# Batch 2's last three units: k, q and u transposed by transfers as well, with a new order of all work

## The chip, the cores and the metric

The kernel runs on one core of a Trainium2 chip. The metric is the device time of one execution in microseconds (us), here the median of three runs: 161.28 us before, from 160.6 to 162.63. The profile is of one further execution.

## The reference

Two layers follow each other. The first is a gated linear attention over 4 batches, 8 heads, 768 tokens and 48 channels; its state is a 48 x 48 matrix for each head. The second takes its output as x of 768 tokens by 384 channels and mixes tokens by a rank of 32, then channels by a hidden layer of 1536:

```python
for t in range(S):
    state = alpha[:, :, t, :, None] * state + np.einsum('bhd,bhe->bhde', k[:, :, t], v[:, :, t])
    y[:, :, t] = np.einsum('bhd,bhde->bhe', q[:, :, t], state)
...
h = xt @ U @ V
u = x + h.transpose(0, 2, 1)
ch = np.maximum(u @ w_ch1, 0.0) @ w_ch2
return (u + ch).astype(np.float32)
```

Inputs and output are float32; the kernel multiplies in bf16.

## The kernel before

**Tiling.** The 768 tokens of a batch are cut into six chunks of 128; a unit is one chunk with all heads, or, in batch 0 and in the first four units of batch 1, a pair of chunks with half of the heads. Batches are counted from 0, so the third batch is batch 2. All units of batches 2 and 3 are of the plain kind (`stage_gla`).

**A plain unit.** Four loads of 192 KB bring alpha, k, q and v (L339). ACT takes the logarithm of alpha (L534), PE sums it along the tokens by a triangular matrix (L541, with totals at L543), and ACT makes the running product and its inverse (L551, L552). DVE or POOL multiply k and q by them (L562) into one `rkq` buffer of bf16. The products are then transposed, since the scores need channels on the partitions. Normally PE does it (L576, four transposes for k and four for q, into PSUM) and DVE or ACT copy the result into a `kqt` buffer (the copies are recorded in the helper, L273 and L275). For units in `QUEUE_T`, all six of batch 3, one transposing transfer on SP's queue goes from `rkq` to `kqt` instead (L588). Then come scores (L604), the causal mask on DVE (L614), the state's new term (L627), its addition on DVE (L654) and scaling (L638), and y from old state and masked scores (L666, L671), for which v has been cast to bf16 (`rv`, L277 or L273). y is copied into `xb`.

**After the six units of a batch** (`stage_mix`): the low-rank mix (L686, L716) and u = x + h on DVE (L717). The hidden layer needs u with channels on the partitions. For batches 1 and 2 PE transposes it for two chunks at a time (L736, six transposes) and DVE or ACT copy it out. For batches in `QUEUE_U`, only batch 3, a transposing transfer does it for two chunks (L722); u then lies chunk by chunk, and `u_half` gives the first layer three pieces of 128 columns where it has one of 384 otherwise. The hidden layer is `mlp1` (L767, relu at L777 and L779) and `mlp2` (L793, addition of u at L799), after which the output is stored (L802, L804).

**Order.** No planner runs on the chip or at build time: `TABLE` lists all groups of instructions in one order, three characters each, two for the number of the group and one for its engine (P, A, D, G for POOL, S for SP). Each engine and SP's queue execute their own entries in this order, waiting where data or a buffer is missing. `SLOTS` gives the buffers, in the order of first use. An entry `++x` issues so many matmuls on a filler, to warm PE; the table before has none. All loads, stores and transposing transfers are issued by SP.

**Buffers.** There are 40 `io` buffers for loads and results, 4 `rkq`, 4 `kqt`, 5 `rv`, and 8 banks of PSUM.

Of the kernel before, what the change touches and what calls it, by code (L numbers as in the profile page):

```python
# [13 lines left out]

CODE = "ABCDEFGHIJKLMNOPQRSTUVWXYZabcdefghijklmnopqrstuvwxyz0123456789+-"
TABLE = """
A8SCcACePCfABISBASCzAC1PA9SBQSETAEVPCiDCkPA+SCgACjDClPCnDDjADlPC2ABDSCmDC3AEXAC0GA-SCdGC4ADmACoPCqDDoACrPChACsDBBSC5GDCP
DDDDnAABSCpDEWAC7PC9ACvPCtPCuDDEPBCSC6GC8PC+DBESDKAAFGAGPAHAAJPAKAEYADFDC-PDBDDADDMPDOADNACwPCyADPABJSDpGDrPBMSBKSDtDDGP
DqGDZPBSSEaGDsPDuDBFSEcPEeDDHPDIDDvPDwDDxDBHSDLADQGDSPDyPDUDD8ACxAD+PBLSDkADzPD0DDJADaPDbDBRSEZGEbPEdDBYSG2ABGSDRGEAAD-A
BUSGfAG4PG6ABTSEUAEBAG5AD1PD2DDcPDdDDTPDVDBNSECGD3PEfPEhDGhPGiAEgDGkABOSEDGBPSD9GD4PBVSGlGBWSGjAGmGBgSBcSBXSGgGAASADGBZS  # L20
G8GAQSARGAMSANGAOSAPGAeSAfGEiPD5PD7AG7AD6AEjPEkDDWPDXDDYDDfPAgSELPEmPDePEEPEGDAhGEFPElPEHAEMPENDAiSAjGEnPEpDEoAHmABbSG3G
AUSAVGBaSG9GBiSASSATGAWSBkSBdSDgPDhDDiAHNAEIPEJDBoSGnPGpAEOPEPPEKDBfSHoPHqAHtGHrABeSHpAAYSBhSAaSAcSAmSAoSAqSBqSBjSBpSAkS
BmSBlSBnSAuSAwSAsSAySA2SA4SBrSGoPGqDHPPEQPERAESAGuPGvDGwDGrPGtDGsDEqPACSBySA6SA0SEwPErPEzPE8PE5PEtPEsAE9PE+AE6PE7AE2PFHP
EuPEvAE3PE4DE0PE1AExPEyDG+PFJPFDPE-PFjPHAAGxGFFPFKDHRAFNPHQAHSAFkDFGDFlPFBPFCDFIDFnPFoAFfPFgAF5PF6DFdPFOAFmAFEDFADFeDFhP
GyPFiAF3PBwSB0SG-PHBAF1PBsSBuSHFPF4DHGDAXAGzPG1DG0AF2AH-AHCPHEDHDDHHDIVAFLPFMDFTPFUDFRPFSDIBPFtPFuAICAHTGHVPHXAFVPFrPFsA
HJPFWAIFAAdAHOGHvPHxDHcPHdDHKPHLDIXPIYAIZAIDAHMAHeDHfDHUGHWPFpPFqAHYDFPPFQAAZGIEAHsGHuPHwDAbGFZPAnGFxPFyAFaDHyPHZPHbDHaD
H0DHzDFbPFcAIHDAlAFXPFYABvSHiPFvPFzPHhPHIGApGIbGFwAF0AArGALGIdPHjPHlDHkAHnGH1PH2DH3DH4DIaGIfAIcPIeAH6PGTPIJPILDIGGIIPIAA
H7PIKDGNPH8PH+AH9AIMPIODINDIgPIiDIhDGZPAxAF7PIPPAvGAzGAtAGaPH5GIRDGBPHgGITPIQDISDGCPIWAIjPGOPGUPIUAIkAAEGIlPA1GImDF8PA7A
A5AA3AGDPGEDItPIzPI1PI0DB4SBtSF9PIvPIuDF+DKLAI2DIwDGVPInPIpPK0AK2PGPPKfAKNPKRAKQAIxPGWDK3AI3PI4AGbPIoDIqDKhPKkAKiAIrPIyD
JXPJjPGcDIsAKjAKnDKlAGQDJTPJUAJkAI7PJNPJJPJDPJEDKOAKSDK5AK4AI8AKPAKMGKTGJHPI5PJdPI6AK6AJKDJIDJLPJODJYDB2SBxSBzSJMALJAJVP  # L30
JWAJRPJSAK8GKpPKrAJfPLLPLPAK+PLAAKbPJeDB1SKUPKWAK7DJgDB8SLeALNALOALMAJBPKmGKoPKgGKvPKcDKwDKVPKXDI-PJPPJnPJoDJlPJAAJmAK9P
I9PI+AJFPJGAJQALgPLhALjALkAKqDJCDK-DKYPKZDLBPKsPKtDLDDCASB+SLzACBSB9SJZPJaALiAKBPB5SCQSLQDKuDLCDKaDB7SCESGHPJvPL1PJbPLmG
LoPLqDJhPKxDJwPNlANnPB3SK1GLEPLFDJxPGIPLHPJyDJiDGJPGKDOaAL3AJcAL2AL4DNpAB6SLRGLTPLVDNrANoANqALSPLUAB-SLfGCCSCGSNtDKyPKzA
LKALlGLnPJ7PL5GLIDLpDL7PL9AL6PL8ALGGLZPLaDCTSObGKCPLrPLtDLWPLXDL+PCHSNmAKDPKEDLsDLYDKdPKeDJ8PCISN2AN4PN5AN6AN8AN7AOcPOdA
J9PJ+DCFSNsGAIGNyPLbGLxPLuPNzDJpPLvDLwGL-DJ1PCMSCDSL0GCJSGRSLyAOIAOKPKGPOMACLSN3AOgAOOALcPMADMBPLdDMCDJqPNuSCSSN9DNvPNxD
NwDMDPONAJrPKHPMEAMNPOfAOeAMFPMGDMLPMMDCYSOiGCUSO+AJ2PMHPCWSCPSCKSCRSOhGCNSCVSCOSCbSO-GMIDN0PKIPN1AOsAMODMRPMJPMKAMPPMQD
JsDJ3PKJDMTPMUDODPOEDJtSMfPMhPMiDMjPMgAMkAOLAOJAMbPMnPMlPMSDMVPOPDJ4DMWDOuPOwAO0DOyAMcDPAPOxAMXPMYAMxPPBAMoAMyAMdPMeAMvP
OQDNBPCZSNCAM3POVPMwDOFDOWDMZPOvAOzGCXSN+GMpPMqDMaDOnPM9PM+DOXDM1PPCAMmANDPM7PM8AOjSOkPOoDM5PM6AM-PNAANFPNHPCaSM2AOmDOlD
OqPOrDMtPNEDNIPORSOSPMuAN-SOAPOCDOBDM4AMzPM0AOTDNRPMrPMsAOGPOHANSPOUDO1SO2PO3DO4DPEGPDGNGAPFSPGPNMPOpGOtGO5PO6DO7GNJPO8P
O9ANTPOYPOZAPHDJzSGSSPIDPJPPKANbPGLSPLPPMANcPPNPPZPPaDPODNWPPPPPQDPSPPRSPTDNNPPUPPVDPWSNgPNOPNhPPXPNXPGMSPYDPbSNiPNjDNYP  # L40
NZDF-SNdPNeDPsPPiPPoPPyPPzANfSNKDNLSKFSPjDGFSGGSJ5SPePPfAPcPPgPPhAP0PP1APpDNUDJuSNVSNaSP2PP3DQEPPqPPtAQAPQBDQFAP4PPmPPnA
P+PP-APdAJ6SPuPKKSNPDKASNQSPwPQCPPxDQIPPrAGdSPkPPlDP5DGASQRPQWPP8PQMPP6PQDAPvAQXPQSPP7DQbPQNPQTPQUDQVSGeSJ0SQGPQKPQYPQZD
QOPQPDQqPQlPQLAQJAP9DQrPGXSJ-SQmPNkSQaSQQSGYSQHAQsPQtDQuSQnPQoDQcPQpSQgPQdPQeDQfSQhPQiPQjDQkS
"""
SLOTS = """
AAAABCBBDECCADFAEAAFBGBCAHBACGHABBECAIBDABAAFBHJBKBDGDFEBBBBAACLCDMNCGCODEPFDHDBCQCAEFACHRDACDDSGTAUACVBBCWEABEXBFCGAAAB
YZBDaCbBcdeAfAghijHCBEGBAkCDBHBFEBlCmDnACDEBFAGHCGFCCEHDADDICJKLNOQPMRSTUVWXYZacbdBAGFAAHBADefgCEGFBAADHGFBDEACABGAAAFEA
CEHACGhiEFjkBDCABBHEBBCGBACFBBEDHDGBEBBAFAEDACADABHAEFBDGEHCAACFlCBHAAECFGBBBCBDHAACBFEBGBACCFDGBBCAAAGBmCAGBnABDAACBDCG
CBCCHBADACBHEBBFFBCAFHBDACADECHGBGHBCFADDEGBABBICAJABBHFEDCAEABCDEGACACFDAHEGABCKNCLOBAFQMCPRGBECBACHBBDTCABASUACCDAVCBD
BEWBXaADCABHGDEDCAYCDACGBBECZEdAfCGABAFCbgDABABGBCAHcjDiBBDChBBDAEAlDCACEAAAECCeCACFkBnGIHJKAEAACFCEQRAFAEGADBDAEFGBMDAA  # L50
CCBHAGBANEHABGCTBADDHACFCBGADAFDVBGBBAHDGBACCEBCAGABCCBHCCEFBDGAAFBGBHAAFGAAHGAWOXHAGFBLBDAFYGEBAFHGEPACHGDBAGFCaEFZfDBg
cFj
"""


# [91 lines left out]
def kernel(  # L147
# [13 lines left out]
    B, H, S, D = q.shape  # L161
# [16 lines left out]
        return [const.tile(shape, dtype, name=f"{name}{i}") for i in range(n)]  # L178

    PAIRS = {0: 3, 1: 2, 2: 0, 3: 0}  # L180
    QUEUE_T = tuple((3, c) for c in range(6))
    LAST, CUT = 3, 240
    QUEUE_U = (3,)
    P = Plan()
    nc.scalar.preload_act_table_set("natural_log_exp_and_others")

# [160 lines left out]
    def xk(b, xb, c):  # L347
        return [(xb, c, 0), (xb, c, 1)] if paired(b, c) else [(xb, c)]
# [182 lines left out]
    def stage_gla(b, c, sprev, xb):  # L531
# [37 lines left out]
        kT, qT = Part(kqT, 0), Part(kqT, 1)  # L569
        if (b, c) not in QUEUE_T:  # L570
            tk, tq = Buf(bank), Buf(bank)
# [12 lines left out]

        if (b, c) in QUEUE_T:
            P.add(
# [93 lines left out]
    def stage_mix(b, xb, ub, uT):  # L680
# [33 lines left out]
        for c in range(NC):  # L714
            hb = Buf(bank)
            P.add({"PE": mm(DM)}, lambda e, c=c, hb=hb: nc.tensor.matmul(hb()[:, 0:DM], lhsT=(ve_sb if paired(b, c) else vm_sb)[:, c * C : (c + 1) * C], rhs=utx(), start=True, stop=True), r=[utx, ("ve" if paired(b, c) else "vm", c // NT)], w=[hb])  # L716
            P.add({"DVE": 465}, lambda e, c=c, hb=hb: nc.vector.tensor_tensor(ub()[:, c, :], xb()[:, c, :], hb()[:, 0:DM], op=ALU.add), r=[hb] + xk(b, xb, c), w=[(ub, c)])  # L717
            if b in QUEUE_U:
                if c % 2 == 1:
# [28 lines left out]
    def u_half(uT, ct, tt, by_chunk):  # L748
        if not by_chunk:
            return uT()[:, ct, tt * TW : (tt + 1) * TW]  # L750
        flat = uT().rearrange("p j t -> p (j t)")
        return flat.rearrange("p (c j t) -> p c j t", c=NC, j=NCT)[:, tt * NT : (tt + 1) * NT, ct, :]

    def mlp1(b, uT, h1, tt):
        for jt in range(NJ):
            hb = Buf(bank)

            if b == 0:
                need = [(uT, tt, j) for j in range(NCT)]
            elif b in QUEUE_U:  # L760
                need = [(uT, "c", c) for c in ((0, 1), (1, 2))[tt]]
# [3 lines left out]
            def f(e, jt=jt, hb=hb):  # L765
                for ct in range(NCT):
                    nc.tensor.matmul(  # L767
                        hb()[:, 0:TW], lhsT=w1_sb[:, ct, jt * 128 : (jt + 1) * 128],
                        rhs=u_half(uT, ct, tt, b in QUEUE_U), start=(ct == 0), stop=(ct == NCT - 1),
                    )  # L770
# [87 lines left out]
```

## Time and profile before

| | |
|---|---|
| median of three runs | 161.28 us (160.6, 161.28, 162.63) |
| profiled execution | 162.81 us, its span 161.0 us |
| TensorE clock granted | full in the span |
| busy: PE, DVE, ACT, POOL | 150.4, 110.1, 90.4, 59.4 us |
| DMA: packets, MB | 96964, 31.05 |
| HBM read and written | 23.89 and 4.72 MB, 178 GB/s |

The span runs from the first to the last instruction recorded; the execution's time has what lies around it as well. A row of the list of groups has line, engine, operation, tiles, shapes and count, then busy time and the mean of one, then the engine's idle time ahead of such instructions with what ended it. A matmul's busy time (some 320 ns for 384 columns) contains its passage through the array; matmuls follow each other faster, so their own share is read from the chain, where consecutive groups are laid end to end. "SPq" is SP's queue: the time in which it is issuing a transfer. "Landing" is from a transfer's issue to its completion.

### The profile page before, as it was taken

The page shows a single profiled execution, that of the slowest core. Times are in us where ns is not written, and L with a number is a line of the kernel's source. Part 1 is how long each engine was busy: PE and PEld are TensorE (multiplying, and loading weights), DVE is VectorE, ACT ScalarE, POOL GpSimd, SP SyncE. Part 2 cuts the span into 40 slices and gives each one's busy share as a digit, 9 for nine tenths or more (in the row PEclk, how much of TensorE's full clock was granted, in tenths as well). Part 3 has the DMA queues.
Part 4 walks back from the last instruction along what each step waited for, and adds up shares of the span by engine and source line. Part 5 has one row for each costly group of instructions (what it writes and reads, how often), then busy time and mean ns, then how long its engine had stood idle before and what let it go on. Part 6 is the DMA issues. An engine that isn't in the chain of part 4 may idle for free.

```text
span 161.0 us, 4539 instructions
## 1 busy us (share of the span) xinstructions
PE 150.4 (93%) x1740; PEld 100.6 (62%) x1740; DVE 110.1 (68%) x242; ACT 90.4 (56%) x233; POOL 59.4 (37%) x95
## 2 busy tenths in 40 slices
PE   0599999999999999999999899999999999999991
PEld 0386877666657655667667575766566566556561
DVE  6157898789768819576888996898868358341431
ACT  4476978766687264989875475468434301560300
POOL 8087686766785321053088431213902000000000
PEclk9999999999999999999999999999999999999999
DMA  5999999898999999899979999878661047751274
GB/s 138 268 299 279 261 278 239 254 310 217 289 249 270 220 222 217 166 210 223 216 154 201 176 183 216 172 155 154 122 125 30 0 93 200 238 162 44 83 235 147
DMA packets 96964, 31.05 MB, mean 193 GB/s; under 512 B 90640, under 2 KB 96912, under 8 KB 96944
## 3 DMA queue, kind: packets, MB, share of 16 engines
q1 hardware_dynamic: 96944, 30.78, 81.6%
q8 instruction: 13, 0.21, 0.6%
q14 instruction: 7, 0.06, 0.1%
HBM read 23.89 MB, written 4.72 MB: 178 GB/s over the span
## 4 chain that ended last, share of the span: by engine, by line
PE 61%; DMA 13%; SPq 11%; DVE 6%; ACT 4%; issue 2%; POOL 0%; DVEq 0%; ACTq 0%; POOLq 0%
PE ps L793 25%; PE ps L767 21%; SPq L332 11%; DMA io<-in_k_dram 4%; DMA io<-in_v_dram 3%; DMA io<-in_alpha_dram 3%; DMA io<-in_moe_w_ch_dram 3%; PE ps L604 2%; PE ps L716 2%; PE ps L671 2%; PE ps L541 1%; PE ps L736 1%; ACT h1t L777 1%; DVE pm L446 1%; PE ps L686 1%
## 5 line engine op out<-in xcount | busy, mean ns | idle before, releaser
L793 PE MATMUL ps<-w_sb,h1t 128*128 128x384 bf16 (+2 forms) x300 | 54.0, 319 | 0.0
L767 PE MATMUL ps<-uT,w_sb 128*128 128x384 bf16 x288 | 52.2, 326 | 0.1
L777 ACT ACTIVATE h1t<-ps 128x384 bf16<-128x384 f32 x62 | 28.5, 497 | 29.0 <-PE ps L767 28.9
L767 PEld LDWEIGHTS <-w_sb 128*128 128x128 bf16 x288 | 26.7, 98 | 16.5 <-ACT w_sb L273 0.4
L793 PEld LDWEIGHTS <-h1t 128*128 128x128 bf16 x300 | 27.0, 97 | 15.9 <-issue 1.0
L779 DVE TENSOR_SCALAR h1t<-ps 128x384 bf16<-128x384 f32 x34 | 17.9, 553 | 9.9 <-PE ps L767 9.9
L799 DVE TENSOR_TENSOR io<-ub,ps 128x384 f32<-128x384 bf16 (+2 forms) x25 | 13.2, 535 | 9.5 <-PE ps L793 9.0
L614 DVE TENSOR_TENSOR pm<-ps,maskc 128x512 bf16<-128x512 f32 x28 | 17.7, 684 | 2.3 <-PE ps L604 2.3
L717 DVE TENSOR_TENSOR ub<-xb,ps 128x384 bf16<-128x384 bf16 x24 | 12.2, 549 | 5.4 <-PE ps L716 5.4
L446 DVE TENSOR_TENSOR pm<-ps,maskp 128x512 bf16<-128x512 f32 x20 | 12.9, 686 | 2.7 <-PE ps L435 1.4
L562 POOL TENSOR_TENSOR rkq<-io,aa 128x384 bf16<-128x384 f32 x9 | 8.3, 926 | 17.3 <-ACT aa L552 7.3
L277 POOL CAST rv<-io 128x384 bf16<-128x384 f32 x15 | 8.4, 558 | 14.0 <-DMA io<-in_v_dram 14.0
L273 ACT CAST xb<-ps 128x192 bf16<-128x192 f32 (+1 forms) x23 | 8.5, 390 | 5.2 <-PE ps L671 4.3
L275 DVE COPY kqt<-ps 128x512 bf16<-128x512 bf16 x22 | 9.1, 419 | 3.0 <-PE ps L411 2.9
L562 POOL TENSOR_TENSOR rkq<-io,ai 128x384 bf16<-128x384 f32 x8 | 7.6, 951 | 7.6 <-DMA io<-in_q_dram 5.3
L277 POOL CAST w_sb<-io 128x384 bf16<-128x384 f32 x16 | 8.0, 505 | 5.8 <-DMA io<-in_moe_w_ch_dram 5.8
L273 ACT COPY kqt<-ps 128x512 bf16<-128x512 bf16 x14 | 8.0, 598 | 3.3 <-PE ps L576 1.7
L393 POOL TENSOR_TENSOR rkq<-io,ai 128x384 bf16<-128x384 f32 x9 | 8.2, 911 | 4.4 <-DMA io<-in_k_dram 2.3
L371 PE MATMUL ps<-lt,upto 128*128 128x384 bf16 x10 | 4.1, 410 | 5.9 <-ACT lt L362 5.8
L534 ACT ACTIVATE lt<-io 128x384 bf16<-128x384 f32 x14 | 7.2, 535 | 3.0 <-DMA io<-in_alpha_dram 3.0
L411 PE MATMUL ps<-ident,rkq 128*128 128x128 bf16 x80 | 8.8, 251 | 0.0
L638 POOL TENSOR_TENSOR st<-sm,tot 128x384 bf16<-128x384 f32 x5 | 4.1, 828 | 12.5 <-DVE sm L654 12.5
(113 smaller groups left out, 232.0 us busy)
## 6 DMA issues: line engine op xcount, KB each, us to landing
io<-in_alpha_dram SPq DMA_DIRECT2D x24, 192.0 KB, 3.7
io<-in_k_dram SPq DMA_DIRECT2D x24, 192.0 KB, 3.7
io<-in_q_dram SPq DMA_DIRECT2D x24, 192.0 KB, 4.0
io<-in_v_dram SPq DMA_DIRECT2D x24, 192.0 KB, 3.9
io<-in_moe_w_ch_dram SPq DMA_DIRECT2D x24, 192.0 KB, 3.9
out_dram<-io SPq DMA_DIRECT2D x13, 192.0 KB, 1.9
out_dram<-io SPq DMA_DIRECT2D x20, 96.0 KB, 2.2
out_dram<-io SPq DMA_DIRECT2D x1, 120.0 KB, 1.7
```

The lines of the kernel that those rows point to most:

```text
L273: nc.scalar.copy(dst, src)
L277: nc.gpsimd.tensor_copy(dst, src)
L332: lambda e: nc.sync.dma_start(t().rearrange("p (h j) d -> p h (j d)", j=2), src[b, hs, sl, :].rearrange("h (p j) d -> p h (j d)", j=2)),
L446: nc.vector.tensor_tensor(dst, s2, maskp.to_broadcast([C, 2, 2, C]), op=ALU.mult)
L562: eng.tensor_tensor(dst()[:, :, 0:D], a(), x(), op=ALU.mult)
L614: nc.vector.tensor_tensor(pm()[:, :, par, :], s2, maskc.to_broadcast([C, HP, C]), op=ALU.mult)
L717: P.add({"DVE": 465}, lambda e, c=c, hb=hb: nc.vector.tensor_tensor(ub()[:, c, :], xb()[:, c, :], hb()[:, 0:DM], op=ALU.add), r=[hb] + xk( ...
L767: nc.tensor.matmul(hb()[:, 0:TW], lhsT=w1_sb[:, ct, jt * 128 : (jt + 1) * 128], rhs=u_half(uT, ct, tt, b in QUEUE_U), start=(ct == 0), sto ...
L777: nc.scalar.activation(dst, hb()[:, 0:TW], AF.Relu)
L779: nc.vector.tensor_scalar_max(dst, hb()[:, 0:TW], 0.0)
L793: nc.tensor.matmul(hb()[:, 0 : hi - lo], lhsT=h1()[:, jt, c * C : (c + 1) * C], rhs=w2_sb[:, jt, lo:hi], start=(jt == 0), stop=(jt == NJ - 1),
L799: P.add({"DVE": 468}, lambda e, hb=hb, lo=lo, hi=hi: nc.vector.tensor_tensor(flat(ou)[:, lo:hi], ub()[:, c, lo:hi], hb()[:, 0 : hi - lo], ...
```

## The change

The units 3, 4 and 5 of batch 2 join `QUEUE_T`, and batch 2 joins `QUEUE_U`. For these PE's transposes and the copies out of PSUM are gone, and six more transposing transfers are issued by SP: three from `rkq` to `kqt`, three from `ub` to `uT`. The first hidden layer of batch 2 reads u by chunks. The order of all groups and the buffers are new throughout, and four warming matmuls stand in it, all among its first 40 entries.

```diff
 TABLE = """
-A8SCcACePCfABISBASCzAC1PA9SBQSETAEVPCiDCkPA+SCgACjDClPCnDDjADlPC2ABDSCmDC3AEXAC0GA-SCdGC4ADmACoPCqDDoACrPChACsDBBSC5GDCP
...
+BQSA8SCcAETACePBISDjADlP++BA9SCfACiDCkPDoA++CA+SBDSChACgACjDClPCnDBASDmACzAC1PCmDCoPC4ABJSBKSA-SCdGCrPC3ABCSC6DC0GEVP++B
...
-    QUEUE_T = tuple((3, c) for c in range(6))
+    QUEUE_T = tuple((b, c) for b in (2, 3) for c in range(6) if b == 3 or c > 2)
     LAST, CUT = 3, 240
-    QUEUE_U = (3,)
+    QUEUE_U = (2, 3)
```

Read out of the tables, SP's queue has these entries, one after the other, around the new transfers (b is the batch, T and U are the transposing transfers for k with q and for u, the figure is the unit, for U the second of its two chunks):

```
before, entries 103 to 112:  v b3.0 | alpha b3.1 | k b3.0 | alpha b3.2 | v b2.5 | k b3.1 | store | v b3.1 | T b3.0 | q b3.3
after, entries 100 to 112:   k b2.5 | q b3.0 | v b3.0 | k b3.0 | alpha b3.3 | T b2.4 | T b2.5 | T b2.3 |
                             k b3.2 | alpha b3.4 | v b2.5 | T b3.0 | k b3.1
after, entries 117 to 124:   q b3.4 | U b2.1 | U b2.3 | v b3.2 | q b3.3 | U b2.5 | q b3.2 | k b3.4
before, entries 126 to 131:  T b3.3 | q b3.5 | T b3.2 | T b3.1 | T b3.4 | T b3.5
after, entries 126 to 136:   q b3.5 | k b3.5 | T b3.2 | T b3.3 | v b3.3 | T b3.4 | T b3.1 | v b3.4 | T b3.5 |
                             store | v b3.5
```

PE's entries ahead of y of unit 5 of batch 2 (the group of L666 and L671) are in number:

| PE's groups ahead of it | before | after |
|---|---|---|
| transposes of k and q in plain units | 16 | 10 |
| `mlp1` groups of three matmuls | 48 | 48 |
| `mlp2` groups of four matmuls | 30 | 27 |
| state's new term in plain units (L627) | 7 | 6 |
| all other groups | the same | the same |
| warming matmuls | 0 | 4 |

## The prediction

> **What bounds the kernel now.** I read the page first: busy shares, the slices, the chain that ended last.
>
> ```profile
> span 161.0 us, 4539 instructions
> ...
> PE 150.4 (93%) x1740; PEld 100.6 (62%) x1740; DVE 110.1 (68%) x242; ACT 90.4 (56%) x233; POOL 59.4 (37%) x95
> ...
> PE   0599999999999999999999899999999999999991
> ...
> DMA  5999999898999999899979999878661047751274
> ...
> PE 61%; DMA 13%; SPq 11%; DVE 6%; ACT 4%; issue 2%; POOL 0%; DVEq 0%; ACTq 0%; POOLq 0%
> ```
>
> PE is full from the third slice to the last but one, so a removed matmul should be worth its own time. But the DMA row is as full as PE's until slice 28, about 112 us. Two resources are at their limit together for two thirds of the span. The windows, by stage, say the same:
>
> ```profile
> 0.00:6.00 6.00, 1.14 (x9) 0.87 (x10) 2.74 (x24) 2.71 (x4) 3.27 (x15) 1.00 0.67 169
> 6.00:60.00 54.00, 52.27 (x814) 36.97 (x813) 39.81 (x89) 38.64 (x105) 33.91 (x52) 1.00 1.01 263
> 60.00:112.00 52.00, 51.28 (x547) 34.53 (x545) 42.65 (x84) 36.02 (x95) 16.94 (x22) 1.00 0.99 189
> 112.00:134.00 22.00, 21.91 (x221) 13.38 (x219) 14.43 (x26) 6.32 (x15) 5.26 (x7) 1.00 0.38 77
> 134.00:158.00 24.00, 23.78 (x159) 14.84 (x156) 10.24 (x21) 6.70 (x15) 0.00 (x0) 1.00 0.56 169
> ```
>
> The columns are stretch, length, busy time of PE, PEld, DVE, ACT and POOL, then granted clock, DMA share and GB/s. From 6 to 112 us the DMA share is 1.0; only then does it fall to 0.38. The clock is full throughout. PE goes in the order of the list, so a load that lands after PE has reached its reader stops PE even where other work would be ready.
>
> **What is removed.** PE loses six groups of four k/q transposes and three groups of six u transposes.
>
> ```profile
> 64.10 0.69 PE ps L736 x12
> ...
> 65.68 0.36 PE ps L736 x6
> ...
> 72.38 0.22 PE ps L576 x4
> ...
> 91.86 0.65 PE ps L793 x4
> ...
> 93.69 0.17 PE ps L627 x4
> ...
> 97.15 0.20 PE ps L671 x8
> ```
>
> In the chain a k/q group takes 0.22 us and a u group 0.36 (12 matmuls take 0.69, so 0.345 to 0.36). The sum is 6 x 0.22 + 3 x 0.345 = 1.32 + 1.03 = 2.35 us of PE time. PE is at its limit there, so that is the most that the removal itself can give.
>
> Nine evacuations go as well:
>
> ```profile
> L275 DVE COPY kqt<-ps 128x512 bf16<-128x512 bf16 x22 | 9.1, 419 | 3.0 <-PE ps L411 2.9
> L273 ACT COPY kqt<-ps 128x512 bf16<-128x512 bf16 x14 | 8.0, 598 | 3.3 <-PE ps L576 1.7
> L275 DVE COPY uT<-ps 128x768 bf16<-128x768 bf16 x3 | 1.7, 556 | 0.7 <-PE ps L736 0.7
> L273 ACT COPY uT<-ps 128x768 bf16<-128x768 bf16 x3 | 2.4, 799 | 0.2 <-PE ps L736 0.2
> ```
>
> At 0.42 or 0.60 us six times, and 0.56 or 0.80 three times, that is 4.2 to 6.0 us of DVE and ACT. Neither bounds this stretch (42.65 and 36.02 of 52 us), so I cost it at nothing. What it could give is the wait that PE has on DVE around 90 us, in this row:
>
> ```profile
> 88.00:92.00 4.00, 3.55 (x57) 2.48 (x55) 3.97 (x8) 2.42 (x6) 2.43 (x3) 1.00 1.34 201
> ```
>
> There DVE is full and PE lacks 0.45 us; that is the bound, from nothing to -0.45.
>
> The first layer now reads batch 2's u by chunks. Batch 3 does so in the kernel before:
>
> ```profile
> 104.14 2.92 PE ps L767 x18
> ...
> 134.35 9.75 PE ps L767 x60
> ```
>
> Batch 2's matmuls (the upper row) and batch 3's (the lower) both take 0.162 us each: nothing. The four 512-column warming matmuls stand among the first entries of the list, where PE works 1.14 of 6 us: nothing; if that cover failed they would cost about 0.22 us each, an estimate from 0.162 us for 384 columns, together 0.9.
>
> **What is added.** Six transfers on SP's queue, three for k and q and three for u. Before has nine of that kind:
>
> ```profile
> L588 SPq DMA_TRANSPOSE kqt<-rkq x6: 1232/1256/2921, 89.4 to 117.2; - x6
> ...
> DMA to landing us min/median/max: 3.1/3.2/4.8
> ```
>
> ```profile
> L722 SPq DMA_TRANSPOSE uT<-ub x3: 1232/1252/1264, 129.4 to 132.7; - x3
> ...
> DMA to landing us min/median/max: 2.8/2.8/2.8
> ```
>
> On a quiet queue each holds SP for 1.25 us and lands after 2.8 to 3.2. Most of the nine run after 109 us, when the queue is quiet. The one that ran amid the loads is the interesting one:
>
> ```profile
> 83.96 0.73 SPq L339 DMA_DIRECT2D io<-in_k_dram  x1
> 84.79 1.13 SPq L339 DMA_DIRECT2D io<-in_alpha_dram  x1
> 86.01 0.87 SPq L339 DMA_DIRECT2D io<-in_v_dram  x1
> ...
> 88.58 0.54 SPq L339 DMA_DIRECT2D io<-in_v_dram  x1
> 89.36 2.92 SPq L588 DMA_TRANSPOSE kqt<-rkq  x1
> ...
> 106.32 1.97 SPq L588 DMA_TRANSPOSE kqt<-rkq  x1
> ```
>
> It held SP for 2.92 us, where loads beside it hold it for 0.54 to 1.13, and it is the one with the landing of 4.8. The transfers' own rate fell with it:
>
> ```profile
> 84.00:88.00 4.00, 4.00 (x60) 3.04 (x58) 2.89 (x7) 2.05 (x7) 3.24 (x6) 1.00 1.04 207
> 89.40:94.20 4.80, 4.35 (x76) 3.13 (x75) 4.77 (x10) 2.47 (x8) 1.03 (x2) 1.00 1.05 147
> 94.20:98.20 4.00, 4.00 (x58) 2.66 (x55) 3.49 (x8) 2.35 (x8) 1.27 (x2) 1.00 1.15 223
> ```
>
> 147 GB/s against 207 and 223 around it: over 4.8 us some 0.33 MB were not moved, about 1.5 us of the stream, beside the 0.26 MB that the transposition itself is. So among loads one costs from 1.25 to 2.92 us of SP's queue. The second that had loads close by, at 106.32, took 1.97. I take 2.0 and keep both ends.
>
> By the Trainium skill, "Advanced Engine Details and Errata", section "X-Bar Transpose (TRN2)", transposing transfers are as fast as ordinary ones, some 90% of a plain copy. By that rule the three would cost what their bytes cost, near 1.25 us; the trace agrees on the quiet queue and not at 89.36 us (2.92).
>
> **Where it lies on the path.** In the new list the three k/q transfers are the 105th to 107th entry of SP's queue: behind them wait the loads of k and alpha of two units of batch 3, and then v of batch 2's last unit. In both lists 106 loads are ahead of that v; in the new one also the three transfers. Before, it was issued at 86.01 and used by the L671 group of the chain at 97.15, 11 us later. That distance is what shrinks, from both sides.
>
> PE gets there sooner: counting the groups ahead of this one in both lists, the new has the six k/q groups less (1.32), three mlp2 groups less, which now come behind it (3 x 0.65), and one group of L627 less (0.17): 3.4 us. Unhindered PE is there at 97.15 - 3.4 = 93.7.
>
> The v gets there later:
>
> ```profile
> io<-in_v_dram SPq DMA_DIRECT2D x24, 192.0 KB, 3.9
> ...
> L277 POOL CAST rv<-io 128x384 bf16<-128x384 f32 x15 | 8.4, 558 | 14.0 <-DMA io<-in_v_dram 14.0
> ```
>
> Issue at 86.0 + 3 x 2.0 = 92.0, landing after 3.9, cast 0.5: usable at 96.4, so PE stands **2.7 us**. At 1.25 us apiece it is usable at 94.2 (0.5 us late); at 2.92 at 99.2 (5.5 us late). The readers of the transposed k and q of units 3 and 5 stand 3.4 and 3.1 us of PE work ahead of the same point and fall in the same wait, since their transfers take the places from 83.96 on (the 105th entry before), 2 us apart, and land 3.2 to 4.8 later.
>
> The transfers' own waits: unit 5's needs the kqt buffer that unit 1 frees 9.2 us of PE work before the point, unit 3's that of unit 0, 8.4 before, so at about 84.9 and 85.5; their turns on SP come at 83.96 + 1.25 = 85.2 or later. Unit 5's k is the 100th load, four ahead; its scaled copy is there some 0.6 us before its turn. I cost both at nothing; if the scaling is late, every load behind waits on SP, since SP goes in order.
>
> The u transfers: the first two must land before the first layer of batch 2. In the new list 4.7 us of PE work lie between the last sum they need and that layer; 0.16 + 0.55 for sum and addition plus a landing of 2.8 to 4.8 gives 3.5 to 5.5. Cost 0, at most 0.8. They hold SP while they wait for the additions, and the loads of batch 3 (v of unit 2, q of unit 3) wait behind them; batch 3 has room for that as long as v of its last unit arrives. That v is now issued behind the last k/q transfer: 1.25 + 0.5 + 3.9 + 0.5 = 6.15 us after it, against 6.0 us of PE work between the buffer that starts the transfer and its reader. Cost 0, at most 1.0 with a slower landing.
>
> **The sum.** On the profiled execution (162.81 us, of which the span is 161.0): -2.35 + 2.7 = +0.35, so 163.2 and a span of 161.4. The median of the runs, 161.28, is 1.5 lower than that execution; I put the difference on the median: **161.6 us**. The three runs lie between 160.6 and 162.63, so 2% (3.2 us) is about what a measurement of this kernel can tell from no change.
>
> **The rivals.**
> *The transfers cost no more than on a quiet queue.* Then 1.25 apiece, a stall of 0.5: 161.28 - 2.35 + 0.5 = 159.4. For it speak seven of the nine transfers, which took near 1.25; against it that the one at this very place in the stream was the slow one.
>
> *The queue in front of the loads decides (slower).* All three take 2.92 and land in 4.8: a stall of 5.5, and with the u transfers' 0.8 and the last v's 1.0 a total of 7.3 - 2.35 = +5, or 166.3. The place is SP's queue ahead of batch 2's last v; it loses time from 1.9 us a transfer on (stall 2.35) and more than 2% from a total stall of 5.6, that is at 2.9 us a transfer, or 2.4 with the two late terms. For it: the row at 89.36, and a DMA share of 1.0 up to 112 us, which leaves no gap to catch up in. Against it: the loads' own issue times are partly back-pressure, which three transfers in a row may share.
>
> *The new order is better at the start as well.* PE lacks 4.9 us in the first 6 and 1.7 in the next 54. If the new order of loads wins 1.4 of these 6.6 and rival one holds: 158.0. Nothing in the profile says which way a new order goes; it can as well lose as much.
>
> **How the numbers follow.** Forecast (160.2 to 163.3): 0.45. Quiet-queue price (158.4 to 160.2): 0.24. Queue decides (163.3 to 167): 0.24, two thirds of it above 164.5. Better start (below 158.4): 0.07. Faster by over 2% is below 158.05: most of the last, and a little of the second, 0.08. Slower by over 2% is above 164.5: 0.17, and 0.03 for a wait that I did not find: 0.20. The rest, 0.72, is within 2%. The range from 158.6 to 165.2 leaves out about 0.08 below and 0.12 above.
>
> **What would show it.** PE's matmuls fall by 42 less the four warming ones, to 1702, and the L576 and L736 rows shrink to 40 and 18. The three k/q transfers of batch 2 show 1.3 to 2.9 us on SP, and the load rate dips beside them. PE has an idle gap of 2 to 3 us between 86 and 97, released by DVE masks behind a transfer or by the cast of v; later PE is full to the end. I am wrong on the price if the three take 1.25; wrong on the mechanism if PE has no gap there and the time is lost or won before 60 us or after 112, in batch 3.

## The result, and the profile after

The changed kernel takes 163.7 us (median of 6 runs, 163.39 to 164.78). The kernel before, beside it on the same chip, takes 162.36 (6 runs, 160.6 to 163.15). The ratio is 1.0101, with a 95% interval from 1.0058 to 1.0144: about 1% slower, and within the 2% that counts as no change. The ratios leave out executions that lie over 1.5% above the fastest of their kernel; the medians are of all. The forecast was 161.6 on a median of 161.28, a ratio of 1.002. Of the 2.1 us between 161.6 and 163.7, 1.1 are the other median before; on 161.28 the measured ratio gives 162.9. The profiled execution took 164.25 us with a span of 162.5, against 162.81 and 161.0 before. Lines of the kernel behind the list of groups are one lower than in the kernel before (L686 is L685, L588 is L587).

The page of the changed kernel: span, busy time, the rows of the slices, the shares of the chain.

```profile
span 162.5 us, 4443 instructions
...
PE 149.0 (92%) x1702; PEld 96.9 (60%) x1702; DVE 109.8 (68%) x236; ACT 85.9 (53%) x225; POOL 63.0 (39%) x100
...
PE   0798798999998999999999799999999999999992
...
DMA  4999997997999999899979999889999136675334
...
PE 56%; DMA 20%; SPq 16%; ACT 3%; issue 2%; POOL 1%; DVE 0%
```

The 1702 matmuls are there as foretold. PE's slices now have a 7 in the 23rd, 89.4 to 93.4 us, and are looser in the first eight; the chain has more DMA (20% for 13) and more of SP's queue (16% for 11).

The same windows as before, and one of 4 us around the new gap:

```profile
6.00:60.00 54.00, 50.76 (x810) 34.70 (x809) 41.27 (x87) 40.26 (x115) 31.84 (x49) 1.00 0.98 258
60.00:112.00 52.00, 50.33 (x498) 32.12 (x497) 39.59 (x77) 29.96 (x79) 20.51 (x26) 1.00 1.02 190
92.00:96.00 4.00, 2.69 (x33) 1.63 (x30) 3.18 (x7) 0.52 (x1) 1.11 (x2) 1.00 1.02 189
112.00:134.00 22.00, 21.61 (x224) 13.46 (x221) 13.46 (x25) 7.80 (x18) 7.36 (x10) 1.00 0.78 146
134.00:158.00 24.00, 24.00 (x152) 14.72 (x151) 11.80 (x24) 5.23 (x12) 0.00 (x0) 1.00 0.54 150
```

PE lacks 3.24 us from 6 to 60 (1.73 before), 1.31 us from 92 to 96, and 0.39 from 112 to 134. The last 24 us are as full as they can be. The clock is full throughout.

What stands at each gap is told by the waits on the instructions themselves. First the queue of SP (start, duration; the three rows of L587 from answers that show them singly), then PE and POOL:

```profile
83.92 0.69 SPq L338 DMA_DIRECT2D io<-in_alpha_dram  x1
84.78 1.79 SPq L587 DMA_TRANSPOSE kqt<-rkq  x1
87.28 1.23 SPq L587 DMA_TRANSPOSE kqt<-rkq  x1
88.61 1.28 SPq L587 DMA_TRANSPOSE kqt<-rkq  x1
89.94 0.58 SPq L338 DMA_DIRECT2D io<-in_k_dram  x1
90.58 0.64 SPq L338 DMA_DIRECT2D io<-in_alpha_dram  x1
91.27 1.63 SPq L338 DMA_DIRECT2D io<-in_v_dram  x1
```

```profile
93.58 0.40 PE L603 MATMUL ps<-kqt 48*128 48x128 bf16 x8 [1.31 <-DMA kqt<-rkq]
...
95.62 0.50 POOL L276 CAST rv<-io 128x384 bf16<-128x384 f32 x1 [2.88 <-DMA io<-in_v_dram]
```

The three k/q transfers (units 4, 5, 3, in this order) take 1.79, 1.23 and 1.28 us of SP. Between the first, which ends at 86.57, and the second, at 87.28, SP stands 0.7 us. The third lands 4.92 us after its issue (the chain below), and the scores of unit 3 wait for it: PE stands 1.31 us and goes on at 93.58. The last v is usable at 96.1, and its reader comes after that: v is not what PE waits for.

In the chain this is the place where it leaves PE:

```profile
87.89 0.72 POOL rkq L561
88.61 4.92 DMA kqt<-rkq
...
93.58 0.40 PE ps L603 x8
...
117.14 4.42 DMA kqt<-rkq
...
121.60 0.40 PE ps L603 x8
```

(The chain puts the issue at 88.61 down to a product of POOL. That one belongs to batch 3 and runs on to 88.80; unit 3's own products on POOL had ended at 86.71, and SP was busy until 88.51 with the transfer ahead. So it is SP's queue that released it.)

Why SP stood is in the row of its waits from 80 to 96 us, and in DVE's rows, whose last is the product of unit 5's k:

```profile
SPq L587 <- DVE rkq L561: 0.6, 1, 0.6
```

```profile
82.83 0.57 DVE L561 TENSOR_TENSOR rkq<-io,ai 128x384 bf16<-128x384 f32 x1
...
84.52 0.54 DVE L653 TENSOR_TENSOR sm<-ps,st 128x384 f32<-128x384 f32 x1
85.10 0.84 DVE L637 TENSOR_TENSOR st<-sm,tot 128x384 bf16<-128x384 f32 x1
85.86 1.27 DVE L561 TENSOR_TENSOR rkq<-io,ai 128x384 bf16<-128x384 f32 x1
```

The product ended at 87.13. DVE had added to and scaled the state of unit 2 ahead of it (L653, L637), since the list said so. And the product itself took 1.27 us, where that of unit 4, of the same form, took 0.57 at 82.83. With 0.57 it would have ended at 86.43, before the first transfer left SP at 86.57. So the hole needs both, the place behind the two instructions and the long product. Why the product is long at this place no run shows.

To see where the time came from, two marks serve: the low-rank mix of batch 1 and that of batch 2 on PE (start, duration), before and then after.

```profile
58.34 0.35 PE L686 MATMUL ps<-xb,ue_sb 128*32 128x384 bf16 x4
...
98.26 0.50 PE L686 MATMUL ps<-xb,u_sb 128*32 128x384 bf16 x6
```

```profile
60.23 0.35 PE L685 MATMUL ps<-xb,ue_sb 128*32 128x384 bf16 x4
...
97.88 0.50 PE L685 MATMUL ps<-xb,u_sb 128*32 128x384 bf16 x6
```

The changed kernel is 1.9 us late at the first mark, 0.4 us early at the second, and 1.5 late at the end (the spans). The work between the marks follows from the two lists and the times of the groups in the chains. Between the marks the changed kernel has 3.6 us less and wins 2.3: six k/q groups (1.32), two `mlp2` groups (1.30), two sums along the tokens (0.24 each), one group of scores (0.33) and one of L626 (0.17). Behind the second it has 1.4 us more and loses 1.9: three `mlp2` groups (1.95), one of scores and one of L626 moved there, and three u groups (1.03) went. Ahead of the first mark the lists differ by 0.2 us (one `mlp2` group less, two sums more), beside the four warming matmuls, which stand where PE waits: the 1.9 us there are waiting, not work.

### The profile page after: what moved, and what is told of

The parts are those of the page before. It is cut to its first block, busy times and chain, and to the rows that moved or that the text cites. A ratio compares the mean times of both kernels' runs of the same rounds, so it can differ in the third digit from the quotient of the medians.

```text
span 162.5 us, 4443 instructions
## 1 busy us (share of the span) xinstructions
PE 149.0 (92%) x1702; PEld 96.9 (60%) x1702; DVE 109.8 (68%) x236; ACT 85.9 (53%) x225; POOL 63.0 (39%) x100
## 4 chain that ended last, share of the span: by engine, by line
PE 56%; DMA 20%; SPq 16%; ACT 3%; issue 2%; POOL 1%; DVE 0%
PE ps L792 25%; PE ps L766 21%; SPq L331 13%; DMA io<-in_moe_w_ch_dram 10%; DMA kqt<-rkq 6%; DMA io<-in_alpha_dram 4%; PE ps L715 2%; SPq L304 1%; PE ps L603 1%; PE ps L540 1%; PE ps L670 1%; ACT h1t L776 1%; PE ps L665 1%; SPq L279 1%; PE ps L685 1%
## 5 line engine op out<-in xcount | busy, mean ns | idle before, releaser
L792 PE MATMUL ps<-w_sb,h1t 128*128 128x384 bf16 (+2 forms) x300 | 54.6, 320 | 0.3 <-DVE h1t L778 0.2
L776 ACT ACTIVATE h1t<-ps 128x384 bf16<-128x384 f32 x59 | 27.3, 493 | 25.2 <-PE ps L766 24.9
L778 DVE TENSOR_SCALAR h1t<-ps 128x384 bf16<-128x384 f32 x37 | 19.3, 552 | 12.9 <-PE ps L766 12.9
L561 POOL TENSOR_TENSOR rkq<-io,aa 128x384 bf16<-128x384 f32 x11 | 10.3, 942 | 11.4 <-ACT aa L551 9.6
L276 POOL CAST rv<-io 128x384 bf16<-128x384 f32 x18 | 9.0, 504 | 14.5 <-DMA io<-in_v_dram 14.5
L561 POOL TENSOR_TENSOR rkq<-io,ai 128x384 bf16<-128x384 f32 x11 | 10.3, 941 | 8.9 <-ACT ai L550 4.7
L637 POOL TENSOR_TENSOR st<-sm,tot 128x384 bf16<-128x384 f32 x7 | 6.0, 854 | 13.9 <-DVE sm L653 13.9
L392 POOL TENSOR_TENSOR rkq<-io,ai 128x384 bf16<-128x384 f32 x9 | 8.5, 946 | 3.9 <-DMA io<-in_k_dram 2.0
L274 DVE COPY kqt<-ps 128x512 bf16<-128x512 bf16 x17 | 7.0, 419 | 4.5 <-PE ps L575 2.4
L410 PE MATMUL ps<-ident,rkq 128*128 128x128 bf16 x80 | 8.0, 229 | 0.7 <-POOL rkq L392 0.4
```

Source lines behind the costliest of these rows:

```text
L276: nc.gpsimd.tensor_copy(dst, src)
L561: eng.tensor_tensor(dst()[:, :, 0:D], a(), x(), op=ALU.mult)
L776: nc.scalar.activation(dst, hb()[:, 0:TW], AF.Relu)
L778: nc.vector.tensor_scalar_max(dst, hb()[:, 0:TW], 0.0)
L792: nc.tensor.matmul(hb()[:, 0 : hi - lo], lhsT=h1()[:, jt, c * C : (c + 1) * C], rhs=w2_sb[:, jt, lo:hi], start=(jt == 0), stop=(jt == NJ - 1),
```

## The experiments

Two ways were tried: put parts of the change back on PE in the new order, and change one thing about the transfers. The runs with a part put back had to have the transposes placed in the list by hand, and that turned out to matter. Each ratio is against the kernel before on the same chip; the runs were made on three chips, four on each, and the changed kernel was not timed again beside them.

**Both kinds of transposes back on PE, new order.**

```diff
-    QUEUE_T = tuple((b, c) for b in (2, 3) for c in range(6) if b == 3 or c > 2)
+    QUEUE_T = tuple((3, c) for c in range(6))
-    QUEUE_U = (2, 3)
+    QUEUE_U = (3,)
```

> The new order with all transposes of batch 2 on PE again (no added transfer). First theory: the changed kernel loses about 1.8 us to the new order of the first 60 us, 1.7 to waits for transposing transfers and wins 2.35 on PE. Then this kernel has the 2.35 back on PE and no wait for transfers: 163.7 + 2.35 - 1.7 = about 164.3, slower than before, and PE reaches the mix of batch 1 near 60.2 us as in the changed kernel. Rival theory, that the transfers alone make the kernel slow and the new order costs nothing by itself: about 162.4, as before.

Measured: 169.44 us, ratio 1.0349 (1.025 to 1.0448). Far from the expectation, and not because of the work: PE waited for copies out of PSUM and for the banks that they free.

```profile
PE ps L576 <- DVE h1t L779: 1.2, 1, 1.2
PE ps L627 <- ACT uT L273: 1.0, 1, 1.0
PE ps L716 <- ACT uT L273: 0.9, 1, 0.9
PE ps L541 <- DVE uT L275: 0.7, 1, 0.7
```

Columns: who waits, for whom, us in total, times, longest. These 3.8 us belong to the places where I put the groups. So the run does not give the price of the new order; it shows that a transpose on PE in a full list costs more than its matmuls when its bank and its copy have no place.

**Only k and q of the three units back on PE, and only u back on PE.** The edits are the first and the second half of the diff above.

> The new order with k and q of the three units on PE again; u still goes by transfers. First theory: PE +1.32, and the wait of 1.6 us at the scores of unit 3 near 92 us is gone: 163.7 + 1.3 - 1.6 = 163.4, no change against the changed kernel. Rival (the k/q transfers hold back loads well beyond that wait): under 162.5.

> The new order with u of batch 2 on PE again; k and q still go by transfers. First theory: the u transfers cost no wait, so PE +1.03 is all: 163.7 + 1.0 = 164.7. Rival (the u transfers hold back the loads of batch 3 and cause its late wait): 163.7 + 1.0 - 0.4 or more, 164.0 or less, and the wait near 121 us is gone.

Measured: 165.8 us, 1.0138 (1.0049 to 1.0228), and 168.42 us, 1.0261 (1.0155 to 1.0366). The second misses both its expectations and has the three waits for copies of u again, 2.6 us. The first is the more telling. The gap at 92 us is gone and v is issued at 86.95, 4.3 us sooner than in the changed kernel, where the three transfers take 5.1 us of SP with the hole. The time lies above both expectations all the same, for then SP stands, in the waits from 80 to 96 us and the window from 88 to 96 of this run:

```profile
SPq L587 <- DVE rkq L561: 6.8, 1, 6.8
```

```profile
88.00:96.00 8.00, 7.58 (x108) 5.38 (x106) 5.75 (x13) 4.19 (x10) 2.35 (x3) 1.00 0.26 52
```

The transfer of batch 3's first unit is at the head of SP's queue and waits 6.8 us for a product of DVE. All loads behind it wait too, and the DMA share falls from about 1.0 to 0.26. A transposing transfer that comes to its turn before its data closes the queue.

**The start of the kernel before.** The first 430 entries of before's list, then all others in the new order; no warming matmuls.

> The first 430 entries in the order of before (no warming matmuls), the rest in the new order, all six transfers kept. First theory: the loss of 1.8 us by the new start is gone, about 161.9, and PE reaches the mix of batch 1 near 58.4 us as before. Rival (the transfers alone are the loss, the start's lag would be made up while PE waits for them anyway): 163.2 to 163.7, with a longer wait near 92 us.

Measured: 171.61 us, 1.0462 (1.0362 to 1.0562). The seam itself made new waits (4.5 us of PE for a logarithm in the plain units, whose alpha came late), and the granted clock of the profiled execution was 0.96 in the mean. So nothing follows on the start.

**Unit 3 alone back on PE.**

```diff
-    QUEUE_T = tuple((b, c) for b in (2, 3) for c in range(6) if b == 3 or c > 2)
+    QUEUE_T = ((2, 4), (2, 5)) + tuple((3, c) for c in range(6))
```

> The changed kernel with k and q of unit 3 of batch 2 alone transposed by PE, in the place of its transfer; the other five added transfers stay. First theory (PE's gap near 92 us is the third transfer of a row of three, issued last and landing late): the gap of 1.3 to 1.7 us goes, PE has 0.44 more, 163.7 - 1.1 = 162.6. Rival (something else is late right behind it, the cast of the last unit's v or the second transfer): the gap only changes its line and the time is 163.5 to 164.3.

Measured: 164.59 us, 1.0155 (1.0093 to 1.0217). The rival holds in kind, no gain, with a time slightly above its range. The gap of 1.3 us fell apart into smaller ones, the longest of 0.6, and the mix of batch 2 stands at 97.95, as in the changed kernel (97.88). Two transfers on SP wait 1.5 us each for products of DVE.

**No warming matmuls.** The four entries for them leave the list.

> The changed kernel without the four warming matmuls. Both theories of the loss (start of the order, waits for transfers) have them beside PE's idle time at the start: no change, 163.2 to 164.2. A rival in which they stand on the path at the start: 162.8; one in which PE's clock needs them: over 164.7.

Measured: 164.5 us, 1.0147 (1.0068 to 1.0226): 0.3 us above the expected range, and no difference from the changed kernel that can be told, since the intervals overlap. Its profile repeats the changed kernel's: marks at 60.42 and 98.01, a wait of 1.3 us for the third transfer, a span of 162.5.

**The kernel before with three transfers that nobody reads.** They go ahead of SP's 105th entry, into free `uT` space:

```diff
+    P.extra = lambda i: nc.sync.dma_start_transpose(spare[i], w1_sb[:, 0, 0:1024])
```

> The kernel before with three more transposing transfers of the k/q size, with nobody reading them, ahead of the 105th entry of SP's queue (where the changed kernel has its three): the price of the transfers in the stream by itself. First theory: SP is held 1.3 to 1.9 us by each, v of batch 2's last unit is issued 4 to 6 us later, near 91, and since the order before uses it only at 97 and has more room still in batch 3, the time stays: plus 0 to 0.5 us. Rival (the transfer stream up to 112 us sets the end of this kernel): plus 3 to 5 us.

Measured: 164.26 us, 1.0128 (1.0056 to 1.02), some 2 us more. In SP's queue:

```profile
82.62 4.80 SPq L270 DMA_TRANSPOSE uT<-w_sb  x3
...
88.81 0.69 SPq L344 DMA_DIRECT2D io<-in_v_dram  x1
```

1.6 us apiece. The v that mattered in the prediction is issued 2.8 us later than before, and PE does not wait for it: its distance of 11 us had that much slack. Even so the time rose, by less than half of what the transfers took: more than the theory's 0.5, less than the rival's 3. In the profiled execution, the fastest of the four, both marks stand as in the kernel before (58.32 and 97.97) and 0.9 us is lost behind the second; the rest it does not show.

**The start of the kernel before, up to the mix of batch 1.** Its first 610 entries, then the new order.

> The first 610 entries in the order of before, past the mix of batch 1 and the first layer of batch 1, the rest in the new order with all six transfers. Theory that the losses add up: the lag of 1.8 us at the mix of batch 1 is gone and so it is at the end, 161.9. Rival theory, that the transfers in SP's queue set when PE goes on near 92 us whatever came before: PE's wait there grows from 1.3 to about 3 us and the time stays at 163.2 to 163.9.

Measured: 165.51 us, 1.0232 (1.016 to 1.0304).

```profile
57.10 0.35 PE L685 MATMUL ps<-xb,ue_sb 128*32 128x384 bf16 x4
...
98.69 0.50 PE L685 MATMUL ps<-xb,u_sb 128*32 128x384 bf16 x6
```

```profile
93.15 2.62 PE ps L792 x8
```

```profile
82.96 6.32 SPq L587 DMA_TRANSPOSE kqt<-rkq  x3
```

```profile
SPq L587 <- DVE rkq L561: 3.7, 2, 2.2
```

The start is 3.1 us ahead of the changed kernel's at the first mark, and 0.8 behind it at the second. My theory, that the start's 1.9 us and the waits simply add, fell; the time is above the rival's range too. Of the 3.9 us lost between the marks, 2.0 are waiting: PE lacks 3.5 us there for 1.5 in the changed kernel, with 1.9 us on k/q transfers (1.3) and 1.0 on a copy of DVE's into `kqt`. Another 1.2 are the clock: from 93.0 to 95.8 us the granted clock was 0.53, and eight `mlp2` matmuls took 2.62 us that take 1.41 elsewhere in the chains (the row by itself). The three transfers leave SP hardly earlier, at 89.3 for 89.9, since transfers wait 3.7 us there for DVE. That pointed at the products, and at the next runs.

**A quarter of the bytes.**

```diff
+            nt = 2 if b == 2 else 8
-... nc.sync.dma_start_transpose(kqT().rearrange("x z e c -> x (z e) c"), ...
+... nc.sync.dma_start_transpose(kqT().rearrange("x z e c -> x (z e) c")[:, 0:nt], ...[:, 0:128 * nt])
```

> The changed kernel, but the three k/q transfers of batch 2 move a quarter of their columns (64 KB for 256 KB); the scores of these units read what earlier units left there, so the numbers of batch 2 are not the reference's; all waits and the order are the same. Theory (the transfers' own time on SP and until they land sets PE's restart near 93.6 us): the last of them is issued near 87.7 instead of 88.6 and lands in 3 us or less, so PE goes on near 90.7; most of the 3.0 us of gap goes: 160.8 to 161.9 us. Rival A (data ready late, or another wait directly behind, as in the runs with one unit less or with the earlier start): 163.0 to 163.8 us, the wait stands at another group.

Measured: 162.75 us, 1.0019 (0.9986 to 1.0051), between the two. SP still needs 6.19 us for the three, since the second waits 1.6 us for DVE, and the last lands 4.41 us after its issue, for 4.92 at full size:

```profile
82.61 6.19 SPq L588 DMA_TRANSPOSE kqt<-rkq  x3
```

```profile
L588 SPq DMA_TRANSPOSE kqt<-rkq x4: 1168/1484/2041, 82.6 to 92.2; - x4
```

```profile
87.60 4.41 DMA kqt<-rkq
```

The middle row has the shortest, the median and the longest that these three and one of full size hold SP, in ns: a quarter of the bytes holds it hardly shorter. Three quarters of the bytes are worth half a microsecond of landing here, 0.9 where the queue is freest (2.3 for 3.2). From mark to mark this run takes 37.10 us (59.37 to 96.47), 0.55 less than the changed kernel, and PE's wait for the third transfer is 0.7 us for 1.3. Its profiled execution also has a first mark 0.9 earlier, which no edit accounts for. So the bytes are worth 0.55 us between the marks, where the next run wins 1.5; how much of the 0.8% between the two ratios is theirs stays open.

**Unit 5's scaled k earlier on DVE.** Its three entries move up in the list; of all engines' orders only DVE's changes by it, by one instruction. Around it (sum and scaling are those of unit 2's state; the expectation calls the scaling a mask):

```
changed kernel:  scaled k b2.4 | ... | sum b2.2 | scaling b2.2 | scaled k b2.5
this run:        scaled k b2.4 | ... | scaled k b2.5 | sum b2.2 | scaling b2.2
```

> The changed kernel with one DVE instruction moved: unit 5's scaled k ahead of the mask and sum of unit 2 (with the load of its k and its ACT exponential named earlier in the list). Theory (SP's stream pins PE: the second transfer waited on SP from 86.1 to 87.1 for this product): the three transfers go without a hole, the third is issued near 87.5 instead of 88.6, PE restarts near 92.5 instead of 93.6; 0.9 to 1.1 us less, 162.6 to 162.8 us. Rival A (the DMA queues are full, so what is issued sooner only lands slower): no change, 163.4 to 164.0 us.

Measured: 162.24 us, **0.9979** (0.9945 to 1.0013), against 1.0101 (1.0058 to 1.0144) of the changed kernel; the intervals do not touch. The two were not timed beside each other. On the chip of this run the nearest to the changed kernel is the run with a quarter of the bytes, which has the late product and 1.0019; against it the gain is 0.4%, and the intervals overlap. So the size in time is known only roughly; where it comes from the profile shows. DVE, SP, and the two marks:

```profile
84.44 0.54 DVE L561 TENSOR_TENSOR rkq<-io,ai 128x384 bf16<-128x384 f32 x1
...
84.44 4.49 SPq L587 DMA_TRANSPOSE kqt<-rkq  x3
...
90.26 1.61 SPq L338 DMA_DIRECT2D io<-in_v_dram  x1
...
60.15 0.35 PE L685 MATMUL ps<-xb,ue_sb 128*32 128x384 bf16 x4
...
96.30 0.50 PE L685 MATMUL ps<-xb,u_sb 128*32 128x384 bf16 x6
```

```profile
88.00:96.00 8.00, 7.77 (x114) 5.50 (x113) 7.73 (x14) 2.69 (x8) 2.24 (x3) 1.00 0.95 179
```

The product takes 0.54 us at its new place and is done at 84.98, the three transfers go nearly without a hole (4.49 us for 5.11), the third is issued at 87.6 instead of 88.6. From 88 to 96 PE lacks 0.23 us (1.31 before the edit), the second mark is 1.6 us sooner with the first one where it was, and the span is 160.9 us for 162.5. The gain (1.6 us of span) is more than the hole on SP (0.7): the transfers that left a little sooner also landed sooner, 3.3 to 3.8 us after their issue instead of 3.2 to 4.9. What PE waits for next is the cast of v, 0.2 us: the wait that the prediction had.

**The same, and two loads of batch 3 put behind the transfers, v directly behind them.** ACT's logarithm of the alpha that is moved goes three places back as well. Entries of SP:

```
changed kernel:  v b3.0 | k b3.0 | alpha b3.3 | T b2.4 | T b2.5 | T b2.3 | k b3.2 | alpha b3.4 | v b2.5
this run:        k b3.0 | T b2.4 | T b2.5 | T b2.3 | v b2.5 | alpha b3.3 | v b3.0 | k b3.2 | alpha b3.4
```

> As the run with the early scaled k, and the loads of alpha of unit 3 and v of unit 0 of batch 3 go behind the three transfers, and v of unit 5 of batch 2 directly behind them, ahead of all loads of batch 3. Theory: the transfers are issued at about 83.4, 85.2 and 86.7 instead of 84.8, 87.1 and 88.6, PE restarts near 91 to 91.7; 1.9 to 2.6 us less: 161.1 to 161.8 us, about the kernel before. Rival A (no gain from the place in the stream): 163.4 to 164.0 us. Rival B (the two loads that were put back come too late for batch 3, and its first units wait): 164.5 us or more.

Measured: 164.86 us, 1.0121 (1.0073 to 1.0168). By the waits it is rival B, by the ratio a time between A and B (some 164.3): the waits for the transfers fall to 0.7 us, and a new one takes their place, the logarithm of batch 3's alphas, which now come late.

```profile
PE ps L540 <- ACT lt L533: 2.8, 2, 1.5
PE ps L603 <- DMA kqt<-rkq: 0.7, 2, 0.4
```

(The profiled execution took 167.1 us, with a lower granted clock, 0.7 to 0.8, in the 24th and 25th of its slices; the kind of wait is read from it, not its size.)

**The changed kernel with three more transfers that nobody reads.** The edit is that of the run on the kernel before, ahead of the three of batch 2.

> The changed kernel with three more transposing transfers of the size of k and q, that nobody reads, directly ahead of the three of batch 2 on SP. In the kernel before, three such transfers at about this place took 4.8 us of SP and 1.3% of the time. Theory (the changed kernel has no slack left in this stream): what they take of SP, 4.3 to 4.8 us, comes nearly whole on the time: PE's gap ahead of 97 us grows by 4 us, 167 to 168.5 us. Rival (there is slack as in the kernel before, or the transfers' wait for data hides it): 164.5 to 166 us.

Measured: 167.77 us, 1.033 (1.0277 to 1.0383), 4.1 us above the changed kernel (3.7 by the ratios), where the same three cost the kernel before some 2. They take 4.52 us of SP, the three of batch 2 follow in 4.05, and PE waits for these:

```profile
83.77 4.52 SPq L269 DMA_TRANSPOSE uT<-w_sb  x3
88.47 4.05 SPq L592 DMA_TRANSPOSE kqt<-rkq  x3
```

```profile
PE ps L608 <- DMA kqt<-rkq: 4.7, 3, 2.8
```

The changed kernel waits 1.7 us for such transfers, so 3.0 are new. Here SP's stream does set the time, for most of what it is held: what the changed kernel has used up is the slack ahead of this point.

## Why the prediction was right or wrong

The time lies in the range and in the class that had most of the chance. As it stands, 163.7 lies in the band of the second rival (163.3 to 167); by the ratio, 162.9, it lies in that of the forecast. The forecast was about 1% too low, and that it came so close is in part luck: a transfer priced too high made up for part of two losses that had been left at nothing.

**The bound** was read rightly: PE and the DMA stream are at their limit together up to 112 us. The run with three more transfers in the changed kernel shows it most plainly. (The 2.9 us a transfer, from which on the second rival has a loss of 2%, is 2.96 by its own sum.)

**The removal, 2.35 us.** The counts are right (1702 matmuls, 40 and 18 of the two transposes). Its worth was not shown by itself: the runs that put the groups back had other waits. What can be said is that the run with the early product, with hardly any wait left between the marks, won 3.8 us there (36.15 us for 39.92), against 3.6 of work less and 0.5 less of waiting. So the k/q groups were worth their time, or nearly.

**Costed at nothing: evacuations, u by chunks, warming.** For the four matmuls the run without them shows no cost. Batch 2's first layer by chunks takes 9.42 us for 57 matmuls on the chain, 0.165 each for 0.162. The gain of up to 0.45 us from the evacuations was not tried alone; in the run with the early product PE lacks 0.23 us from 88 to 96, for 0.45 in the kernel before.

**The price of a transfer, 2.0 us.** Mis-sized: 1.79, 1.23 and 1.28, a mean of 1.43; 1.35 to 1.6 where three go in a row without a long wait in the other runs. The single 2.92 of the kernel before, to which I gave weight because of its place, was not the price of the place: the same transfer, that of batch 3's first unit, took 1.44 in the changed kernel and 1.37 in the kernel before with three more ahead of it. What makes a single one slow no run shows. The rule of the Trainium skill ("Advanced Engine Details and Errata", section "X-Bar Transpose (TRN2)") is that transposing transfers are as fast as ordinary ones. By the time to landing the trace agrees: a median of 3.8 us for the nine k/q transfers of 256 KB and 3.8 for the loads of 192 KB. By the time on SP it does not: a median of 1.28 us for these transfers and 0.59 to 0.69 for the loads. So the 1.25 that the prediction derived from the rule was the number of its quiet rows, and these would have been the better guide here, with the stall of 0.5 of the first rival.

**The transfers' own waits, costed at nothing. In the stretch of the transfers this is the step that failed.** The prediction had unit 5's scaled k there "some 0.6 us before its turn", and said what follows "if the scaling is late". It was late, by 0.6 us. The prediction shows no row for its 0.6 us; what the trace shows is a sum and a scaling ahead of the product on DVE, and the product itself at 1.27 us for some 0.55 elsewhere. Moving that one product takes 1.6 us off the span and 1.2% off the ratio (0.4% against the nearest run on the same chip); by the spans this is about as much as the changed kernel is slower than the one before. A price near that of the quiet queue with this hole is what happened; without the hole the edited kernel comes near the first rival, apart from the start.

**Where PE stands.** A gap between 86 and 97 us was foretold, of 2.7 us, behind v. It was 1.31 us, at the scores of unit 3, behind the third transfer; v itself was issued at 91.27 (92.0 foretold) and usable at 96.1 (96.4), and not waited for. The prediction let the scores "fall in the same wait"; they were the wait. The size was wrong because the transfers were cheaper, the place because the third transfer was reckoned from an earlier issue (83.96 and twice 2.0, some 88.0, and a landing of 3.2 to 4.8); it left at 88.61 and took 4.92 to land.

**The start.** The new order was taken at nothing, with a chance of a better one. It is 1.9 us worse at the first mark, all of it waiting. By its own words the prediction is wrong on the mechanism "if PE has no gap there and the time is lost or won before 60 us or after 112": the gap was there, and more than its length was lost before 60 us as well. How much of this the end feels is open. In the run with before's start up to the mix, the 3.1 us won there were lost again before the second, half of it by waits (for the transfers and for a copy on DVE) and a third by a lower clock, so with the late product it bought nothing; the run with the early product has the late start and is level with the kernel before. Before's start together with the early product was not tried.

**Behind the gap.** The u transfers and the last v were costed at nothing, with bounds of 0.8 and 1.0: no wait of 0.2 us or more on u or on the last v. Right. One wait of 0.39 us was not foretold, for the k/q transfer that lands at 121.6.

**The sum.** Foretold: -2.35 + 2.7 = +0.35. Measured, between the profiled executions: +1.5. By the marks, each stretch against the work that left or joined it, the losses are 2.1 us at the start (0.2 less work, 1.9 later), 1.3 between the marks (3.6 less, 2.3 won) and 0.5 behind (1.4 more, 1.9 lost): -2.35 + 3.9. Of the 1.3, PE's idle time shows 0.8 (1.5 for 0.7), and of the 0.5 it shows 0.3; the other 0.6 us the rows do not explain. At the start the busy time is too rough for such a split: up to the mark it is 51.90 us in the changed kernel and 51.07 in the run with the early product, with the same groups.

## What to carry to other kernels

A transfer that moves from an engine to an in-order queue brings its data's due time with it: before its own price, ask when its last producer runs, what stands ahead of that producer on its engine, and who is behind the transfer in the queue. Here one vector instruction, placed two places too late, cost some 1.6 us of the span through a queue that carries no work of DVE's. And work taken off a full engine is worth its time only where nothing else is full at the same place; two marks in the program, compared between kernels, show quickly in which stretch it was kept and in which given back.

## What was not expected of the hardware

The size of a transposing transfer hardly matters among loads: with 64 KB for 256 KB it held SP hardly shorter and the one that PE waited for landed in 4.41 us for 4.92. The same three transfers cost some 2 us in one kernel and some 4 in the other, at about the same place and the same 4.5 to 4.8 us of SP: what they cost went by the slack that was left. And the same product on DVE took 1.27 us at its late place and 0.54 two instructions earlier.
